# Turning float64 weights into float32 with one fewer VectorE pass, and one subtraction moved from GpSimd to VectorE

## The chip, the cores and the metric

One NeuronCore of a Trainium2 chip runs the whole program. The metric is the time of one execution on the device in microseconds (us), lower is better. The engines are TensorE (PE, with its weight loads listed apart as PEld), VectorE (DVE), ScalarE (ACT), GpSimd (POOL) and SyncE (SP), which here issues all DMAs. Each engine works through its own queue in order; semaphores hold an instruction until what it reads is there.

## The reference

Three parts follow each other: attention with keys and values averaged over 8 positions, a feed-forward layer with a rational function, and a gated feed-forward layer. Batch 8, 8 heads, 576 positions, head size 64, so 4608 tokens of 512 values; hidden sizes 2048 and 1536.

```python
k_p = k.reshape(B, H, Sp, pool, D).mean(axis=3)          # pool = 8, Sp = 72; v_p likewise
scores = scale * np.matmul(q, k_p.transpose(0, 1, 3, 2))
attn = softmax(scores); attn_out = attn @ v_p            # -> x, 4608 x 512
h = x @ w_in                                             # 512 -> 2048
P = a[0] + a[1]*h + a[2]*h**2 + a[3]*h**3
Q = 1.0 + np.abs(b[0])*np.abs(h) + np.abs(b[1])*h**2
x = (P / (Q + 1e-06)) @ w_out                            # 2048 -> 512
gate = 1.0 / (1.0 + np.exp(-(x @ w_gate))); val = x @ w_val
out = (gate * val) @ w_out2                              # 512 -> 1536 -> 512
```

The five weight matrices arrive as float64 (drawn as float32, then multiplied by a float64 scalar). The kernel reads each number as two 32-bit words and makes float32 of it by itself.

## The kernel before

**Precision by two parts.** Every large product is done with each operand split into a high part (fp32r) and a low part (what the rounding lost); a product is three matmuls (`mm3`, L485 to L487). So every weight tile needs a conversion from float64 and then a split.

**Conversion of one weight tile** (128 x 512 float64; the high words are `raw[:, :, 1]`, the low words `raw[:, :, 0]`, so each is read and written with a stride of two words). `conv1a` (ScalarE): L90 multiplies the high word, read as float32, by 2^-112, which brings the exponent into the range that float32 uses; L92 turns the low word into an integer of its top bits. `conv1b`: on VectorE, L98 shifts the result of L90 left by 3 into a scratch tile `wx`, which loses the sign, and L100 (here called the merge) takes the sign bit of the unshifted word and ORs it in; on GpSimd, L102 adds the integer of the low word. `conv2` splits: L117 (ScalarE) copies to the high part, L118 subtracts to get the low part, on GpSimd unless another engine is handed over.

**Who converts what, and when.** The first weights (`wi` from w_in, `wo` from w_out) have 16 tiles each. They are converted while the first 16 steps of the rational layer run: `weights_a(p)` (L748) does at the end of step p the split of `wi` p+3 and of `wo` p, then `conv1a` of `wi` p+5 and `wo` p+2, then loads. `conv1b` of these is put off to `gap()` (L783) in the middle of the next step. `weights_a` also runs in the lead-in steps before step 0, where the first attention tiles are made. The weights of the gated layer are converted in the background in steps 16 to 111 (`background`, L194): 12 units, three conversions each, 36 in all; `conv2` of these stays on GpSimd.

**One step n** (L770 to L794; 144 in all, 16 for each block of 512 tokens): PE computes `h` of one 128-wide slice of the hidden layer (`g1`, 12 matmuls), then attention's `psx`, then the second product of step n-3 (`g2`, 12 matmuls, `acc`), then scores and transposes of attention (`sc`, `pta`). VectorE does `rational1` (L528 to L530), the conversions of `gap()`, `rational3` (L542 to L544) and, for an attention tile, the low part of x (L420), the row maximum and difference (L369, L371) or the sum and its reciprocal (L384 to L387). ScalarE does three functions of h (L525 to L527), the high part of g (L510), Ln and Exp (L536, L538), and then the conversion's L117, L90 and L92. GpSimd does the low part of g (L513), the conversion's L102 and L118, and attention's products (L388, L334, L349). The order on each engine is the order in which the program writes the instructions (`tc.manual_schedule()`).

After step 143 comes the gated layer, which has no conversions.

Of the kernel before, what the change touches and what calls it, by code (L numbers as in the profile page):

```python
# [9 lines left out]
F32 = mybir.dt.float32  # L10
F32R = mybir.dt.float32r
I32 = mybir.dt.int32
U32 = mybir.dt.uint32
AF = mybir.ActivationFunctionType
ALU = mybir.AluOpType
# [20 lines left out]
def attention_moe_glu_kernel(ctx: ExitStack, tc: tile.TileContext, q, k, v, w_in, w_out, ca, cb, w_gate, w_val, w_out2, out):  # L36
    nc = tc.nc
# [24 lines left out]
    scale = 1.0 / math.sqrt(D)  # L62
# [13 lines left out]
    def new_tmp(name, tag="m", bufs=3):  # L76
        return rot.tile([P, 512], F32, tag=tag, name=name, bufs=bufs)
# [6 lines left out]
    def conv1a(*raws):  # L84

        for raw in raws:
            hw, lw = raw[:, :, 1], raw[:, :, 0]


            nc.scalar.activation(hw.bitcast(F32), hw.bitcast(F32), AF.Copy, scale=2.0 ** -112)  # L90

            nc.scalar.activation(lw, lw.bitcast(U32), AF.Copy, scale=2.0 ** -29)  # L92

    def conv1b(*raws):

        ws = [(raw[:, :, 1], raw[:, :, 0], new_tmp("wx").bitcast(I32)[:, :raw.shape[1]]) for raw in raws]
        for hw, lw, x in ws:
            nc.vector.tensor_scalar(out=x, in0=hw, scalar1=3, scalar2=None, op0=ALU.logical_shift_left)  # L98
        for hw, lw, x in ws:
            nc.vector.scalar_tensor_tensor(out=hw, in0=hw, scalar=-2 ** 31, in1=x, op0=ALU.bitwise_and, op1=ALU.bitwise_or)  # L100
        for hw, lw, x in ws:
            nc.gpsimd.tensor_tensor(out=hw, in0=hw, in1=lw, op=ALU.add)  # L102

    between = []
# [1 line left out]
    def conv1(*raws):  # L106
        conv1a(*raws)
        between.append(lambda: conv1b(*raws))
# [6 lines left out]
    def conv2(raw, wh, wl, eng=nc.gpsimd):  # L115
        t = raw[:, :, 1].bitcast(F32)
        nc.scalar.activation(wh, t, AF.Copy)  # L117
        eng.tensor_tensor(out=wl, in0=t, in1=wh.bitcast(F32), op=ALU.subtract)  # L118
# [7 lines left out]
    def slot(tag, dtype, name, pool=None):  # L126
        shape = [P, 2, 4 * P] if dtype is F32R else [P, 4 * P, 2]
        return (pool or wp).tile(shape, dtype, tag=tag, name=name)
# [8 lines left out]
    wi, wo, wi_raw, wo_raw = {}, {}, {}, {}  # L137
# [10 lines left out]

    def wi_conv2(f):
        wi[f] = slot(f"wi{f}", F32R, "wi")  # L150
        conv2(wi_raw.pop(f), wi[f][:, 0], wi[f][:, 1])

    def wo_load(f):
        wo_raw[f] = slot(f"wo{f + 1}", I32, "woraw") if f + 1 < FS else slot(f"st{(f + 1 - FS) % 5}", I32, "woraw", stage)
# [74 lines left out]
    with tc.manual_schedule():  # L229
# [29 lines left out]
        units, raws, loaded = [], {}, [0]  # L259
# [202 lines left out]
        for b in range(1, B):  # L462
            e0, e1 = max(at[first[b - 1]], -2), at[last[b - 1]]
            for c in range(2 * NCH):
                w, f = (("k", pool_k), ("v", pool_v))[c // NCH]
# [282 lines left out]
        def weights_a(p):  # L748

            for ahead, f, n in ((3, wi_conv2, NF1), (0, wo_conv2, NF1), (5, wi_conv1, NF1), (2, wo_conv1, NF1),  # L750
                                (8, wi_load, NF1), (5, wo_load, NF1)):
                if 0 <= p + ahead < n:
                    f(p + ahead)
# [16 lines left out]
        for n in range(N1):  # L770
# [24 lines left out]
            x = n - (N1 - NF1)  # L795
# [79 lines left out]
```

## Time and profile before

| | us |
|---|---|
| median of 3 runs (1896.67 to 1898.65) | 1896.74 |
| profiled execution: its own time | 1894.58 |
| its span, from first to last instruction | 1892.7 |

| engine, whole span | busy us | share |
|---|---|---|
| PE | 1804.6 | 95% |
| PEld | 1564.4 | 83% |
| DVE | 1242.5 | 66% |
| ACT | 943.0 | 50% |
| POOL | 896.4 | 47% |

Busy is the union of an engine's instructions. The shares are means over stages that differ: the first 45 us are attention's lead-in, from there to about 200 us the 16 steps run that convert the first weights, up to about 860 us the steps with background conversions, up to about 1000 us steps without any, and then the gated layer. The tables by stretch, further down, tell the stages apart. In a row of the timeline the first number is the start in us from the start of the span and the second the duration; what follows "out<-in" are the tiles by the names of the program; in brackets stands how long the engine was idle before and what ended that.

### The profile page before, as it was taken

The page shows a single profiled execution, that of the slowest core. Times are in us where ns is not written, and L with a number is a line of the kernel's source. Part 1 is how long each engine was busy: PE and PEld are TensorE (multiplying, and loading weights), DVE is VectorE, ACT ScalarE, POOL GpSimd, SP SyncE. Part 2 cuts the span into 40 slices and gives each one's busy share as a digit, 9 for nine tenths or more (in the row PEclk, how much of TensorE's full clock was granted, in tenths as well). Part 3 has the DMA queues.
Part 4 walks back from the last instruction along what each step waited for, and adds up shares of the span by engine and source line. Part 5 has one row for each costly group of instructions (what it writes and reads, how often), then busy time and mean ns, then how long its engine had stood idle before and what let it go on. Part 6 is the DMA issues. An engine that isn't in the chain of part 4 may idle for free.

```text
span 1892.7 us, 25138 instructions
## 1 busy us (share of the span) xinstructions
PE 1804.6 (95%) x8936; PEld 1564.4 (83%) x8936; DVE 1242.5 (66%) x1847; ACT 943.0 (50%) x1754; POOL 896.4 (47%) x855
## 2 busy tenths in 40 slices
PE   5578999999999999999999999999999999999999
PEld 4467788787777788788887999998998998998997
DVE  7999999999998899988778543343334333333331
ACT  4777777677676777776666422222222222222221
POOL 6768556565564665653224234334235225235231
PEclk9799999999999999999999999999999999999999
DMA  7343355343544553443154574574573664663661
GB/s 247 131 153 120 107 191 187 135 171 135 186 159 156 192 176 137 168 148 119 56 196 150 190 236 153 166 235 133 184 228 123 211 211 129 222 201 112 206 203 43
DMA packets 123117, 312.56 MB, mean 165 GB/s; under 512 B 11504, under 2 KB 43248, under 8 KB 122992
## 3 DMA queue, kind: packets, MB, share of 16 engines
q1 hardware_dynamic: 122992, 310.95, 48.7%
q8 instruction: 71, 1.16, 0.2%
q14 instruction: 54, 0.44, 0.1%
HBM read 257.95 MB, written 52.95 MB: 164 GB/s over the span
## 4 chain that ended last, share of the span: by engine, by line
PE 67%; DVE 21%; ACT 4%; issue 4%; DMA 2%; POOL 2%; SPq 0%; ACTq 0%; POOLq 0%; DVEq 0%
PE h L485 13%; PE h L487 12%; PE h L486 12%; PE acc L485 3%; PE acc L487 3%; PE acc L486 3%; PE accA L722 3%; PE accA L723 3%; PE h L722 3%; PE h L723 3%; PE accA L721 3%; PE h L721 3%; DVE u L528 3%; PE psx L413 3%; DVE y L544 3%
## 5 line engine op out<-in xcount | busy, mean ns | idle before, releaser
L658 DVE TENSOR_TENSOR t<-h,t 128x384 f32<-128x384 f32 x360 | 200.7, 557 | 387.0 <-ACT t L666 276.2
L513 POOL TENSOR_TENSOR g<-y,g 128x512 fp32r<-128x512 f32 x144 | 190.6, 1324 | 245.7 <-ACT g L510 186.7
L711 POOL TENSOR_TENSOR t<-t 128x384 f32<-128x384 f32 x72 | 84.4, 1172 | 448.9 <-issue 253.7
L485 PE MATMUL h<-xs,wi 128*128 128x512 f32 x576 | 234.4, 407 | 11.8 <-DVE xs L420 5.2
L485 PE MATMUL acc<-g,wo 128*128 128x512 f32 x576 | 232.8, 404 | 2.2 <-ACT g L510 2.2
L487 PE MATMUL h<-xs,wi 128*128 128x512 f32 x576 | 229.3, 398 | 3.0 <-DVE xs L420 3.0
L486 PE MATMUL h<-xs,wi 128*128 128x512 f32 x576 | 229.2, 398 | 0.0
L487 PE MATMUL acc<-g,wo 128*128 128x512 f32 x576 | 226.0, 392 | 2.4 <-POOL g L513 2.4
L486 PE MATMUL acc<-g,wo 128*128 128x512 f32 x576 | 225.0, 391 | 0.0
L487 PE MATMUL h<-xS,wq 128*128 128x384 f32 x576 | 193.1, 335 | 0.0
L485 PE MATMUL h<-xS,wq 128*128 128x384 f32 x576 | 192.9, 335 | 0.0
L486 PE MATMUL h<-xS,wq 128*128 128x384 f32 x576 | 192.7, 335 | 0.0
L528 DVE SCALAR_TENSOR_TENSOR u<-s,coef,u 128x512 f32<-128x512 f32 x144 | 132.1, 918 | 32.2 <-ACT u L526 31.9
L485 PE MATMUL h<-xA,wq 128*128 128x384 f32 x432 | 149.0, 345 | 0.0
L544 DVE SCALAR_TENSOR_TENSOR y<-u,y 128x512 f32<-128x512 f32 x144 | 143.9, 999 | 4.9
L487 PE MATMUL h<-xA,wq 128*128 128x384 f32 x432 | 144.7, 335 | 0.0
L486 PE MATMUL h<-xA,wq 128*128 128x384 f32 x432 | 144.6, 335 | 0.0
L485 PEld LDWEIGHTS h<-xs,wi 128*128 128x128 f32 x576 | 111.3, 193 | 39.1 <-DVE xs L420 4.2
L525 ACT ACTIVATE s<-h 128x512 f32<-128x512 f32 x144 | 85.0, 590 | 110.4 <-PE h L487 110.3
L542 DVE SCALAR_TENSOR_TENSOR u<-u,h 128x512 f32<-128x512 f32 x144 | 98.5, 684 | 56.0 <-ACT h L538 54.3
L487 PEld LDWEIGHTS h<-xs,wi 128*128 128x128 f32 x576 | 111.1, 193 | 27.9 <-DVE xs L420 3.5
L485 PEld LDWEIGHTS acc<-g,wo 128*128 128x128 f32 x576 | 108.5, 188 | 27.9 <-ACT g L510 2.6
(122 smaller groups left out, 4300.2 us busy)
## 6 DMA issues: line engine op xcount, KB each, us to landing
wq<-w2d SPq DMA_DIRECT2D x252, 512.0 KB, 4.3
wo<-wod SPq DMA_DIRECT2D x88, 512.0 KB, 3.8
w2d<-wq SPq DMA_DIRECT2D x36, 512.0 KB, 2.9
x2d<-o SPq DMA_DIRECT2D x36, 256.0 KB, 2.4
out_dram<-o SPq DMA_DIRECT2D x36, 256.0 KB, 2.0
raw<-in_k_dram SPq DMA_DIRECT2D x32, 256.0 KB, 2.8
raw<-in_q_dram SPq DMA_DIRECT2D x32, 256.0 KB, 2.7
raw<-in_v_dram SPq DMA_DIRECT2D x32, 256.0 KB, 3.1
```

The lines of the kernel that those rows point to most:

```text
L485: nc.tensor.matmul(out_, wl, xh, start=start, stop=False, skip_group_check=on)
L486: nc.tensor.matmul(out_, wh, xh, start=False, stop=False, skip_group_check=on)
L487: nc.tensor.matmul(out_, wh, xl, start=False, stop=stop, skip_group_check=on)
L513: eng.tensor_tensor(out=g[:, 1], in0=y, in1=g[:, 0].bitcast(F32), op=ALU.subtract)
L525: nc.scalar.activation(s, h, AF.Square)
L528: nc.vector.scalar_tensor_tensor(out=u, in0=s, scalar=coef[:, 5:6], in1=u, op0=ALU.mult, op1=ALU.add)
L542: nc.vector.scalar_tensor_tensor(out=u, in0=u, scalar=ONE, in1=r, op0=ALU.add, op1=ALU.mult)
L544: nc.vector.scalar_tensor_tensor(out=y, in0=u, scalar=-2.0, in1=y, op0=ALU.add, op1=ALU.mult)
L658: nc.vector.tensor_tensor(out=out_, in0=a, in1=b, op=ALU.add)
L721: nc.tensor.matmul(a[t], gh, wt[:, 0], start=(f == 0), stop=False)
L722: nc.tensor.matmul(a[t], gh, wt[:, 1], start=False, stop=False)
L723: nc.tensor.matmul(a[t], gl, wt[:, 0], start=False, stop=(f == NF2 - 1))
```

## The change

The multiplication on ScalarE (L90) becomes a leaky one, `Prelu`, with alpha 2^32: positive numbers get the factor 2^-112 as before, negative ones 2^-80. The exponent field of a negative result then has one more bit set, two places below the top; the shift by 3, which pushes out the old sign, moves that bit into the sign's place. So the shift alone gives the right word, and it is done in place: the merge (the old L100) and the scratch tile `wx` go. This holds for all 68 conversions, 32 of the first weights and 36 in the background. Apart from that, `wi_conv2` hands `nc.vector` to `conv2`: the low parts (L118) of the 16 `wi` tiles are computed on VectorE, not on GpSimd. Those of `wo` and of the background stay.

```diff
-            nc.scalar.activation(hw.bitcast(F32), hw.bitcast(F32), AF.Copy, scale=2.0 ** -112)
+            nc.scalar.activation(hw.bitcast(F32), hw.bitcast(F32), AF.Prelu, scale=2.0 ** -112, alpha=2.0 ** 32)
             nc.scalar.activation(lw, lw.bitcast(U32), AF.Copy, scale=2.0 ** -29)
     def conv1b(*raws):
-        ws = [(raw[:, :, 1], raw[:, :, 0], new_tmp("wx").bitcast(I32)[:, :raw.shape[1]]) for raw in raws]
-        for hw, lw, x in ws:
-            nc.vector.tensor_scalar(out=x, in0=hw, scalar1=3, scalar2=None, op0=ALU.logical_shift_left)
-        for hw, lw, x in ws:
-            nc.vector.scalar_tensor_tensor(out=hw, in0=hw, scalar=-2 ** 31, in1=x, op0=ALU.bitwise_and, op1=ALU.bitwise_or)
-        for hw, lw, x in ws:
+        ws = [(raw[:, :, 1], raw[:, :, 0]) for raw in raws]
+        for hw, lw in ws:
+            nc.vector.tensor_scalar(out=hw, in0=hw, scalar1=3, scalar2=None, op0=ALU.logical_shift_left)
+        for hw, lw in ws:
             nc.gpsimd.tensor_tensor(out=hw, in0=hw, in1=lw, op=ALU.add)
...
     def wi_conv2(f):
         wi[f] = slot(f"wi{f}", F32R, "wi")
-        conv2(wi_raw.pop(f), wi[f][:, 0], wi[f][:, 1])
+        conv2(wi_raw.pop(f), wi[f][:, 0], wi[f][:, 1], nc.vector)
```

In the changed file two empty lines more stand ahead of L90, so its Prelu is L92, its low-word copy L94, its shift L100; L102 and all later numbers are as before.

What VectorE has in a row in one step with both conversions, before (step 2; `wiraw` and `woraw` are raw tiles of w_in and w_out, `wx` the scratch tile):

```order
L528 SCALAR_TENSOR_TENSOR u<-s,coef,u 128x512
L529 TENSOR_TENSOR y<-h,y 128x512
L530 SCALAR_TENSOR_TENSOR y<-y,coef,h 128x512
L98 TENSOR_SCALAR wx<-wiraw 128x512
L100 SCALAR_TENSOR_TENSOR wiraw<-wiraw,wx 128x512
L98 TENSOR_SCALAR wx<-woraw 128x512
L100 SCALAR_TENSOR_TENSOR woraw<-woraw,wx 128x512
L542 SCALAR_TENSOR_TENSOR u<-u,h 128x512
L543 SCALAR_TENSOR_TENSOR y<-y,coef,h 128x512
L544 SCALAR_TENSOR_TENSOR y<-u,y 128x512
```

The same place of VectorE in the changed program:

```order
L118 TENSOR_TENSOR wi<-wiraw,wi 128x512
L528 SCALAR_TENSOR_TENSOR u<-s,coef,u 128x512
L529 TENSOR_TENSOR y<-h,y 128x512
L530 SCALAR_TENSOR_TENSOR y<-y,coef,h 128x512
L100 TENSOR_SCALAR wiraw<-wiraw 128x512
L100 TENSOR_SCALAR woraw<-woraw 128x512
L542 SCALAR_TENSOR_TENSOR u<-u,h 128x512
L543 SCALAR_TENSOR_TENSOR y<-y,coef,h 128x512
L544 SCALAR_TENSOR_TENSOR y<-u,y 128x512
```

The two merges are gone, the two shifts (now L100) stand side by side, and the low part of a `wi` tile comes in at the end of the step before, right ahead of L528.

GpSimd at the end of step 1 and in step 2, before (L388 is attention's product, L513 the low part of g):

```order
L388 TENSOR_TENSOR e<-e,r 64x576
L118 TENSOR_TENSOR wi<-wiraw,wi 128x512
L118 TENSOR_TENSOR wo<-woraw,wo 128x512
L513 TENSOR_TENSOR g<-y,g 128x512
L102 TENSOR_TENSOR wiraw<-wiraw 128x512
L102 TENSOR_TENSOR woraw<-woraw 128x512
```

The same place of GpSimd in the changed program:

```order
L388 TENSOR_TENSOR e<-e,r 64x576
L118 TENSOR_TENSOR wo<-woraw,wo 128x512
L513 TENSOR_TENSOR g<-y,g 128x512
L102 TENSOR_TENSOR wiraw<-wiraw 128x512
L102 TENSOR_TENSOR woraw<-woraw 128x512
```

Only the subtraction of `wi` is gone there; nothing else moved. The order on PE, ScalarE and SyncE is that of before, instruction for instruction; ScalarE has its two table loads (L232 and L696) at the same places.

## Rows read from the trace of the kernel before

**Rows 1.** Busy time by stretch: us, then each engine's busy us (instructions).

```profile
core 0: us, PE busy (x) PEld busy (x) DVE busy (x) ACT busy (x) POOL busy (x), PEclk, DMA share, GB/s
...
60.00:200.00 140.00, 106.58 (x471) 86.56 (x472) 137.79 (x179) 100.03 (x178) 103.99 (x91) 0.87 0.37 126
215.00:860.00 645.00, 624.90 (x3023) 512.16 (x3022) 586.85 (x885) 460.57 (x859) 388.43 (x403) 1.00 0.45 162
860.00:1000.00 140.00, 139.87 (x660) 115.95 (x659) 111.20 (x168) 89.82 (x157) 43.46 (x32) 1.00 0.35 124
```

**Rows 2.** The chain that ended last, 60 to 200 us, by line.

```profile
by line: DVE wx L98 17.3%; DVE woraw L100 13.0%; DVE y L544 8.4%; DVE u L528 8.2%; DVE wiraw L100 8.0%; DVE y L530 6.9%; DVE y L543 6.2%; DVE y L529 6.1%; DVE u L542 5.5%; issue 5.3%; DVE e L371 2.5%; DVE kp L317 2.0%; DVE r L384 1.9%; DVE 
```

**Rows 3.** VectorE's groups, 17 to 205 us: xcount | busy us, mean ns | idle before.

```profile
L544 DVE SCALAR_TENSOR_TENSOR y<-u,y 128x512 f32<-128x512 f32 x16 | 23.6, 1474 | 0.6
L100 DVE SCALAR_TENSOR_TENSOR woraw<-woraw,wx 128x512 int32<-128x512 int32 x16 | 21.7, 1358 | 0.5
L98 DVE TENSOR_SCALAR wx<-wiraw 128x512 int32<-128x512 int32 x16 | 18.9, 1179 | 0.5 <-ACT wiraw L90 0.5
L100 DVE SCALAR_TENSOR_TENSOR wiraw<-wiraw,wx 128x512 int32<-128x512 int32 x16 | 16.8, 1049 | 0.5
L98 DVE TENSOR_SCALAR wx<-woraw 128x512 int32<-128x512 int32 x16 | 12.8, 800 | 0.0
```

**Rows 4.** Lines 98 and 100 by themselves: duration in ns, min/median/max, and starts.

```profile
L98 DVE TENSOR_SCALAR wx<-woraw x16: 416/422/2223, 37.5 to 191.0; 128x512 int32<-128x512 int32 x16
...
L100 DVE SCALAR_TENSOR_TENSOR wiraw<-wiraw,wx x16: 693/695/2028, 22.4 to 166.6; 128x512 int32<-128x512 int32 x16
```

**Rows 5.** Timeline around 113 us, VectorE and GpSimd.

```profile
112.64 1.30 POOL L118 TENSOR_TENSOR wi<-wiraw,wi 128x512 fp32r<-128x512 f32 x1
...
112.97 1.25 DVE L98 TENSOR_SCALAR wx<-wiraw 128x512 int32<-128x512 int32 x1
...
113.90 1.49 POOL L118 TENSOR_TENSOR wo<-woraw,wo 128x512 fp32r<-128x512 f32 x1
...
114.25 1.68 DVE L100 SCALAR_TENSOR_TENSOR wiraw<-wiraw,wx 128x512 int32<-128x512 int32 x1
```

**Rows 6.** Timeline around 50 us, VectorE and GpSimd.

```profile
49.72 0.31 POOL L335 TENSOR_TENSOR vp<-raw 64x64 f32<-64x64 f32 x1
50.00 1.28 POOL L118 TENSOR_TENSOR wi<-wiraw,wi 128x512 fp32r<-128x512 f32 x1
50.10 6.25 DVE L544 SCALAR_TENSOR_TENSOR y<-u,y 128x512 f32<-128x512 f32 x1
...
54.51 1.29 POOL L118 TENSOR_TENSOR wo<-woraw,wo 128x512 fp32r<-128x512 f32 x1
```

**Rows 7.** GpSimd's groups, 17 to 205 us: xcount | busy us, mean ns | idle before.

```profile
L118 POOL TENSOR_TENSOR wo<-woraw,wo 128x512 fp32r<-128x512 f32 x15 | 22.6, 1504 | 0.0
L513 POOL TENSOR_TENSOR g<-y,g 128x512 fp32r<-128x512 f32 x15 | 21.8, 1453 | 10.5 <-DVE y L529 10.5
L118 POOL TENSOR_TENSOR wi<-wiraw,wi 128x512 fp32r<-128x512 f32 x16 | 21.0, 1310 | 0.0
L102 POOL TENSOR_TENSOR woraw<-woraw 128x512 int32<-128x512 int32 x16 | 16.6, 1038 | 9.3 <-DVE woraw L100 8.7 <-ACT coef L768 0.7
```

**Rows 8.** ScalarE's groups: two of 17 to 205 us, and a table load.

```profile
L527 ACT ACTIVATE y<-h,coef 128x512 f32<-128x512 f32 x17 | 13.2, 778 | 0.0
L90 ACT ACTIVATE woraw<-woraw 128x512 f32<-128x512 f32 x16 | 10.7, 671 | 0.0
...
L232 ACT ACT_TABLE_LOAD x1 | 1.3, 1283 | 0.8 <-PEq L851 0.8
```

**Rows 9.** Timeline from step 1 to step 2, ScalarE and VectorE.

```profile
65.55 0.69 ACT L526 ACTIVATE u<-h,coef 128x512 f32<-128x512 f32 x1
...
66.28 0.75 DVE L528 SCALAR_TENSOR_TENSOR u<-s,coef,u 128x512 f32<-128x512 f32 x1
```

**Rows 10.** Who waited for whom, 17 to 205 us: total us, times, longest.

```profile
PE pta L395 <- POOL e L388: 33.4, 6, 12.1
```

## The prediction

> **What bounds the kernel now.** I read the stretches first, since the shares of the whole span mix stages. From 60 to 200 us VectorE is busy 137.79 of 140 us and TensorE 106.58, at a mean granted clock of 0.87; from 215 to 860 us TensorE is busy 624.90 of 645 and VectorE 586.85; without conversions (860 to 1000 us) TensorE is busy 139.87 of 140 [rows 1]. So the change can act in two places: strongly in the first 16 steps, where VectorE has no time left, and weakly in the background steps, where TensorE idles 20.1 us in all. Then the chain: from 60 to 200 us it runs almost wholly over VectorE, and three of its lines are the shift and the merges of the conversion, 17.3 + 13.0 + 8.0 = 38% [rows 2]. The gated layer has no conversions and stays as it is.
>
> Last, I ask why these VectorE instructions take so long. A shift takes 0.42 us and a merge 0.69 when nothing is in the way [rows 4], but in the first steps their means are 0.80 to 1.18 and 1.05 to 1.36 us, and L544, with both inputs in SBUF too, has 1.47 [rows 3]. The timeline shows the cause: L98 arrives at 112.97, while GpSimd is in L118 until 113.94, and ends at 114.22, one free duration after that; GpSimd's next L118 takes 1.49 instead of 1.30; L100 comes at 114.25 and waits that one out [rows 5]. These VectorE instructions and GpSimd's exclude each other. It can be worse: L544 at 50.10 waits through five GpSimd instructions in a row, to 56.35 [rows 6].
>
> On that wait the Trainium skill, "SBUF — State Buffer", section "Who interferes with whom", says that a VectorE instruction with two SBUF inputs, or in a mode that uses both ports, and a GpSimd instruction that reads SBUF exclude each other, and that the second one blocks until the first has finished. It speaks against moving L118: on VectorE it is itself such an instruction. Rows 5 agree with it; rows 6 don't, since there the wait lasts for five. By the rule no wait could exceed one GpSimd instruction, step 0 would have nothing to win from a shorter run, and my slower rival (D) could not occur.
>
> **The change part by part, first 16 steps and lead-in.** All in VectorE time, 17 to 205 us.
>
> 1. Merges out: 21.7 + 16.8 = 38.5 us for 32 [rows 3]. Their waits go with them. Certain.
>
> 2. Low parts of `wi` in: 16 instructions of a form that VectorE doesn't have now; nearest is the merge (two SBUF inputs, one with a stride of two, 512 elements): 0.69 free [rows 4], 1.36 on the mean where it always runs into GpSimd [rows 3]. So 11.0 to 21.8; I take the mean of the `wi` merges, 1.05, as L118 stands behind other work as they do: 16.8 us. It waits for ScalarE's L117, which ScalarE reaches before VectorE has done L542 to L544, so I add no wait. Queued behind it on VectorE is L528 of the next step, and behind that ScalarE's Ln and all of `rational3`; a wait here would move the whole step.
>
> 3. Shifts: 18.9 + 12.8 = 31.7 us now [rows 3]; free they would be 32 x 0.42 = 13.4, so 18.3 us are waiting. The second shift of a step now starts right behind the first, before GpSimd's add of the first tile can start, and GpSimd's run ahead of the first is shorter by one L118 of 1.31 us [rows 7]. I take half: -9 (0 to -18). The destination is now strided. The merge writes with that stride at 0.69 [rows 4], so at worst a free shift costs 0.69: +0.27 x 32 = +8.6. I take 0.42, the row with the same operation and input.
>
> 4. L544: 23.6 - 16 x 0.69 = 12.6 us of waiting now [rows 3]. With the merges gone the two adds and L118 of `wo` stand on GpSimd without gaps, so L544 may find one more add (1.04 us [rows 7]) ahead of it; but L118 of `wi` is no longer there, and the run of rows 6 loses two of its five. I take 0 (-8 to +8).
>
> 5. Prelu in L90's place: Copy takes 0.671 us; the dearest function of one input on this engine takes 0.778, with two operands read per partition [rows 8]. Prelu has none of these, so I take 0.671; at the other end 32 x 0.107 = 3.4 us on an engine busy 100.03 of 140 us [rows 1]. Less than Copy is excluded by nothing in the rows, but no path could use it: 0 to +3. The order shows no new table load.
>
> Sum: -38.5 + 16.8 - 9 + 0 = -30.7 us of VectorE time.
>
> 6. What is late next. ScalarE: step 1 has nothing to give, since L526 ends at 66.24 and L528 starts at 66.28 [rows 9]. TensorE: in six places the transposes wait for attention's L388 on GpSimd, 33.4 us in all [rows 10]; behind L388 stand transposes, scores and the next h, so a step after such a place can shorten by only part of what VectorE saves. I count the one step as lost and half of the six: 4 of 16, a quarter. So 0.75 x 30.7 = 23 us arrive. GpSimd is no bound: it loses 21.0 us [rows 7].
>
> **Background, 215 to 860 us.** 36 merges go. TensorE's idle time there is 20.1 us, against 0.1 in 140 us without conversions, so at most 19.5 can be won. Conversions stand in 3 of 8 steps, and the merge is about 0.69 of the 0.69 + 1.0 us that one takes (1.0 is the mean of the shifts in rows 3): 19.5 x 3/8 x 0.41 = 3 us (0 to 7).
>
> Gain 23 + 3 = 26 us. The profiled execution took 1894.58 us (span 1892.7), 2.2 under the median, so 1868.6 there and 1896.7 - 26 = **1870.7 us** for the median.
>
> **Rivals.**
>
> A, the port takes much back: the waits move instead of going. L118 at 21.8, shifts keep their 18.3, L544 +8: -38.5 + 21.8 + 8 = -8.7, times 0.75 = 6.5 us, 1890. For it: rows 5, where one wait follows another and the loop closes over both engines. Against: GpSimd's own load falls by 21 us, and fewer instructions compete.
>
> B, the in-place shift is slow: +8.6, so 22.1 x 0.75 + 3 = 19.6, 1877. The Trainium skill, "VectorE: DVE Perf Modes", section "What auto-detection actually checks", asks for SBUF operands and matching outer dimensions, not for unit stride, before it takes two elements per cycle; by it the shift stays at 0.42. No row shows a strided destination in that operation.
>
> C, more than forecast: all 18.3 us of the shifts' waits and 8 of L544's go too, and TensorE's clock rises because it idles less: 30.7 + 9 + 8 = 47.7, times 0.75 = 36, and 7 behind: 1854.
>
> D, slower: L118 on VectorE gets behind whole GpSimd runs, as L544 in rows 6. It is then 1.50 (L118 of `wo`) + 1.45 (L513) + 0.69 = 3.64 us each [rows 4, 7], 58 us for 16, against 38.5 gained; with L544 at +8 the sum is +28, and as it stands right on VectorE's path nothing of it is hidden: 1925. It decides from 38.5 / 16 = 2.41 us per L118, that is a wait of 1.7. For it: rows 6. Against: that run follows an instruction on 64 partitions (L335), and in rows 5, with full ones, VectorE gets in after a single one.
>
> E, the change doesn't do what it says: Prelu is missing in the loaded table and each use brings two loads. 68 x 2 x 1.283 [rows 8] = 174 us, 2071. The order has only the two loads of before.
>
> **How the numbers follow.** Chances: forecast (1862 to 1876) 0.58, A 0.14, B 0.10, C 0.11, D 0.06, E 0.01. The range goes from near C's end to near A's: 1856 to 1888; half of A, D, E and a little of C lie outside, 0.17. About 0.2%, 3.8 us, is what a measurement of this kernel can tell from no change. Faster by more: the forecast, B, C and most of A, 0.90. The same: the rest of A, 0.04. Slower: D, E, 0.06.
>
> **What would show it right or wrong.** In the profile after: 32 shifts in the first steps, mean 0.5 to 0.8 us, minimum 0.42 (0.69 would be B); 16 low parts on VectorE at about 1.05 us (3.6 would be D); ScalarE's Prelu at 0.67; the end of the first 16 steps 23 us earlier; VectorE still the busiest of that stretch but with some idle time before L528, put down to ScalarE or TensorE; L544 of step 0 well under 6.25. Wrong would be a gain in the gated layer, a TensorE that is busy 98% in the first steps, or a gain there under 10 us with all durations as said: then the quarter in step 6 was too small.

## The result and the profile after

The changed kernel takes 1864.74 us (median of 4 runs, 1862.82 to 1865.53), the one before beside it 1896.7: a ratio of 0.983, 95% interval 0.9813 to 0.9847, so 32 us less. The prediction was 1870.7. The profiled execution took 1865.44 us, with a span of 1863.6.

The same three stretches as in [rows 1], now of the changed kernel (us, then the busy us of each engine with its instructions, TensorE's granted clock, DMA share, GB/s):

```profile
60.00:200.00 140.00, 120.51 (x559) 98.11 (x560) 125.72 (x185) 108.99 (x197) 93.29 (x85) 0.91 0.42 142
215.00:860.00 645.00, 632.78 (x3092) 521.91 (x3091) 572.52 (x864) 466.05 (x871) 386.64 (x401) 1.00 0.47 166
860.00:1000.00 140.00, 135.10 (x608) 110.72 (x607) 110.13 (x153) 88.27 (x151) 46.36 (x31) 0.98 0.35 121
```

VectorE is no longer busy all the time from 60 to 200 us, and TensorE has 14 us more work in it. Fixed windows cover other work once a kernel is shorter, though, so the two kernels are better cut at the same steps: at the first instruction (L528) of VectorE in step 0, 16 and 112. Before:

```profile
45.85:204.24 158.39, 118.71 (x516) 95.48 (x515) 154.52 (x199) 112.69 (x200) 115.41 (x104) 0.87 0.38 131
204.24:861.06 656.82, 636.06 (x3082) 521.16 (x3082) 597.01 (x902) 469.21 (x875) 393.79 (x407) 1.00 0.46 162
```

After:

```profile
41.95:185.88 143.93, 114.00 (x517) 92.03 (x516) 130.55 (x186) 111.03 (x200) 98.84 (x94) 0.89 0.42 144
185.88:829.57 643.69, 629.71 (x3074) 519.11 (x3075) 574.15 (x866) 467.60 (x875) 391.55 (x407) 1.00 0.47 165
```

Step 16 starts 18.4 us earlier (3.9 of them already at step 0), the 96 steps with background conversions take 13.1 less, and everything behind step 112 takes 2.4 more (the span is 29.1 shorter, not 31.5). The median moved by 32, the profiled executions by 29.1.

VectorE's groups of the changed kernel, 17 to 185 us, which answer to [rows 3] (xcount | busy us, mean ns | idle before):

```profile
L528 DVE SCALAR_TENSOR_TENSOR u<-s,coef,u 128x512 f32<-128x512 f32 x16 | 23.7, 1479 | 11.1 <-ACT u L526 11.0
L544 DVE SCALAR_TENSOR_TENSOR y<-u,y 128x512 f32<-128x512 f32 x16 | 18.8, 1178 | 0.6
L100 DVE TENSOR_SCALAR wiraw<-wiraw 128x512 int32<-128x512 int32 x16 | 13.7, 853 | 0.0
L118 DVE TENSOR_TENSOR wi<-wiraw,wi 128x512 fp32r<-128x512 f32 x16 | 12.7, 791 | 0.0
...
L100 DVE TENSOR_SCALAR woraw<-woraw 128x512 int32<-128x512 int32 x16 | 10.4, 651 | 0.0
```

The row of before that has to stand beside the first of these, and that the prediction left out (17 to 205 us):

```profile
L528 DVE SCALAR_TENSOR_TENSOR u<-s,coef,u 128x512 f32<-128x512 f32 x17 | 14.1, 830 | 2.6 <-ACT u L526 2.6
```

Single durations (ns, min/median/max) of the new shift, of L118 on VectorE, and of the Prelu, answering to [rows 4, 8]:

```profile
L100 DVE TENSOR_SCALAR wqraw<-wqraw x36: 419/1250/1553, 206.4 to 825.3; 128x512 int32<-128x512 int32 x36
L100 DVE TENSOR_SCALAR wiraw<-wiraw x16: 415/513/1458, 21.9 to 153.5; 128x512 int32<-128x512 int32 x16
L100 DVE TENSOR_SCALAR woraw<-woraw x16: 416/420/1697, 37.1 to 173.9; 128x512 int32<-128x512 int32 x16
...
L118 DVE TENSOR_TENSOR wi<-wiraw,wi x16: 632/686/1220, 30.6 to 165.0; 128x512 fp32r<-128x512 f32 x16
...
L92 ACT ACTIVATE wiraw<-wiraw x16: 657/674/692, 19.3 to 146.3; 128x512 f32<-128x512 f32 x16
```

The chain of the changed kernel, 60 to 185 us, by line, which answers to [rows 2]:

```profile
by line: DVE u L528 13.2%; DVE y L544 8.9%; DVE y L530 7.8%; DVE y L529 6.9%; issue 4.7%; DVE woraw L100 4.7%; DVE y L543 4.3%; PE h L485 4.0%; DVE wiraw L100 3.9%; DVE u L542 3.8%; PE h L486 3.8%; PE h L487 3.6%; DVE wi L118 3.5%; PE sc L3
```

The conversion had 38% of the chain and has 12 (4.7 + 3.9 + 3.5). TensorE's matmuls appear in it, and L528 has taken the first place. Why, the timeline of VectorE and GpSimd at the end of step 0 shows (start, duration):

```profile
48.51 0.94 DVE L118 TENSOR_TENSOR wi<-wiraw,wi 128x512 fp32r<-128x512 f32 x1
49.48 5.15 DVE L528 SCALAR_TENSOR_TENSOR u<-s,coef,u 128x512 f32<-128x512 f32 x1
...
48.98 0.65 POOL L335 TENSOR_TENSOR vp<-raw 64x64 f32<-64x64 f32 x1
49.59 1.03 POOL L102 TENSOR_TENSOR wiraw<-wiraw 128x512 int32<-128x512 int32 x1
50.59 1.03 POOL L102 TENSOR_TENSOR woraw<-woraw 128x512 int32<-128x512 int32 x1
51.58 1.28 POOL L118 TENSOR_TENSOR wo<-woraw,wo 128x512 fp32r<-128x512 f32 x1
52.83 1.25 POOL L513 TENSOR_TENSOR g<-y,g 128x512 fp32r<-128x512 f32 x1
```

It is the wait of [rows 6] again: L544 of step 0 has lost it (it takes 0.69 at 46.44), but GpSimd's run behind the 64-partition L335 is still there, four instructions long, and L528 of step 1 falls into it. It ends at 54.63, 0.55 us after the run's last instruction; the wait of [rows 6] also ends 0.55 after the run's (54.51 + 1.29 = 55.80; 56.35).

### The profile page after: what moved, and what is told of

It reads as the page before. It is cut to its first block, busy times and chain, and to the rows that moved or that the text cites. A ratio compares the mean times of both kernels' runs of the same rounds, so it can differ in the third digit from the quotient of the medians.

```text
span 1863.6 us, 25047 instructions
## 1 busy us (share of the span) xinstructions
PE 1794.3 (96%) x8936; PEld 1559.6 (84%) x8936; DVE 1192.5 (64%) x1795; ACT 940.0 (50%) x1754; POOL 873.2 (47%) x839
## 4 chain that ended last, share of the span: by engine, by line
PE 72%; DVE 14%; ACT 5%; issue 3%; POOL 2%; DMA 2%; SPq 0%; ACTq 0%; POOLq 0%; DVEq 0%
PE h L485 14%; PE h L487 13%; PE h L486 13%; PE acc L485 4%; PE acc L487 4%; PE acc L486 4%; PE psx L413 3%; DVE u L528 3%; PE h L722 3%; PE h L723 3%; PE h L721 3%; PE accA L722 3%; PE accA L723 3%; PE accA L721 3%; DVE y L530 2%
## 5 line engine op out<-in xcount | busy, mean ns | idle before, releaser
L513 POOL TENSOR_TENSOR g<-y,g 128x512 fp32r<-128x512 f32 x144 | 187.7, 1304 | 265.6 <-ACT g L510 204.7
L485 PE MATMUL h<-xs,wi 128*128 128x512 f32 x576 | 231.7, 402 | 6.7 <-DVE xs L420 3.8
L487 PE MATMUL h<-xs,wi 128*128 128x512 f32 x576 | 227.0, 394 | 0.3 <-DVE xs L420 0.3
L486 PE MATMUL h<-xs,wi 128*128 128x512 f32 x576 | 227.0, 394 | 0.0
L528 DVE SCALAR_TENSOR_TENSOR u<-s,coef,u 128x512 f32<-128x512 f32 x144 | 140.8, 978 | 49.6 <-ACT u L526 49.2
L544 DVE SCALAR_TENSOR_TENSOR y<-u,y 128x512 f32<-128x512 f32 x144 | 136.3, 947 | 4.9
L485 PEld LDWEIGHTS h<-xs,wi 128*128 128x128 f32 x576 | 109.9, 191 | 31.9 <-DVE xs L420 4.6
L485 PEld LDWEIGHTS acc<-g,wo 128*128 128x128 f32 x576 | 108.5, 188 | 27.9 <-ACT g L510 2.6
L487 PEld LDWEIGHTS acc<-g,wo 128*128 128x128 f32 x576 | 108.6, 189 | 27.6 <-POOL g L513 3.6
```

Of the source, the lines that this page charges most:

```text
L485: nc.tensor.matmul(out_, wl, xh, start=start, stop=False, skip_group_check=on)
L486: nc.tensor.matmul(out_, wh, xh, start=False, stop=False, skip_group_check=on)
L487: nc.tensor.matmul(out_, wh, xl, start=False, stop=stop, skip_group_check=on)
L513: eng.tensor_tensor(out=g[:, 1], in0=y, in1=g[:, 0].bitcast(F32), op=ALU.subtract)
L528: nc.vector.scalar_tensor_tensor(out=u, in0=s, scalar=coef[:, 5:6], in1=u, op0=ALU.mult, op1=ALU.add)
L544: nc.vector.scalar_tensor_tensor(out=y, in0=u, scalar=-2.0, in1=y, op0=ALU.add, op1=ALU.mult)
```

## The experiments

**The two parts apart.** The sign step alone, with L118 of `wi` left on GpSimd:

```diff
-        conv2(wi_raw.pop(f), wi[f][:, 0], wi[f][:, 1], nc.vector)
+        conv2(wi_raw.pop(f), wi[f][:, 0], wi[f][:, 1])
```

> The changed kernel, but with the low parts of wi (L118) left on GpSimd; so it has the sign step alone. Port theory (the first 16 steps are bound by what VectorE's port-sharing instructions and GpSimd's take one after the other): L118 occupies the shared port for 1.31 us on GpSimd and 0.69 on VectorE, so this kernel is slower than the changed one by up to 16 x 0.62 = 10 us, I expect 4 to 8, that is 1869 to 1873. Rival (VectorE's own list of instructions is the bound, as the prediction's sum counts it): VectorE has 12.7 us less to do than in the changed kernel, of which three quarters arrive: 1855.

Measured 1865.88 us, ratio 0.9845 (0.9831 to 0.9858): 1 us above the changed kernel, too little to tell from no difference. And the other part alone, L118 moved in the kernel before:

> The kernel before, but with the low parts of wi (L118) moved to VectorE; merges and scratch tile stay. Port theory: the port gets free of 16 x 0.62 = 10 us and the runs on GpSimd get shorter, so faster than before by 3 to 8 us, 1889 to 1894. Rival (VectorE's list alone): VectorE has 16 more instructions of 0.8 us and up, 12.7 us, three quarters arrive: 1906.

Measured 1900.85 us, ratio 1.0026 (1.0016 to 1.0035): 4 to 5 us slower. So the sign step carries the whole gain, 30 to 36 us, and moving the subtraction is worth nothing beside it. Neither account of the price fits either run: L118 on VectorE takes 0.76 us on the mean in the second run and 0.79 in the changed kernel, so it seldom waits long for GpSimd; but where VectorE is full, as before, even 0.76 seems to be more than its removal from GpSimd gives back.

**First weights and background apart.** The old sign step (Copy, shift, merge) only for the 36 background tiles, then only for the 32 first ones with L118 on GpSimd:

```diff
-            conv1(bg["raw"][r - 2])
+            conv1_old(bg["raw"][r - 2])
...
-            conv1(bg["raw"][2])
+            conv1_old(bg["raw"][2])
```

> The changed kernel, but the 36 background conversions done in the old way (Copy, shift into the scratch tile, merge). The trace after is 18.4 us ahead at step 16 and 31.5 at step 112. If the 13.1 us between come from the background merges, this kernel takes 1875 to 1878. Rival: they come from the state that the first 16 steps hand over (a backlog on TensorE and a lower granted clock, which the trace before shows until 370 us and the trace after doesn't); then it stays within 4 us of the changed kernel, 1865 to 1869.

> The kernel before in the first weights (Copy, merge, L118 on GpSimd), with the changed conversion in the 36 background tiles alone. If the background merges are worth what the traces show between steps 16 and 112, 13 us, it takes 1884; by the prediction's own term, 3 us, 1894; the rival of e3 says 1893 to 1897.

Measured 1877.92 us, ratio 0.9905 (0.9891 to 0.9918), and 1885.04, ratio 0.9943 (0.9931 to 0.9956). The background's merges are worth 13 us by the first and 11 by the second, four times the 3 of the prediction; that they come from a state handed over by the first 16 steps is out. VectorE's groups of the background steps say what it saved; before (204 to 861 us):

```profile
L98 DVE TENSOR_SCALAR wx<-wqraw 128x512 int32<-128x512 int32 x36 | 36.0, 1001 | 0.0
L100 DVE SCALAR_TENSOR_TENSOR wqraw<-wqraw,wx 128x512 int32<-128x512 int32 x36 | 25.5, 708 | 1.2
```

and after (185 to 830 us):

```profile
L100 DVE TENSOR_SCALAR wqraw<-wqraw 128x512 int32<-128x512 int32 x36 | 41.5, 1152 | 0.0
```

36.0 + 25.5 - 41.5 = 20.0 us saved, of which 13.1 arrived.

**What the merge's price is made of.** To tell VectorE's own time from its waits for GpSimd, the changed kernel got, after each of the 68 shifts, a row maximum over the same words into a scratch column that nobody reads: an instruction with one input, as long as a merge.

```diff
             nc.vector.tensor_scalar(out=hw, in0=hw, scalar1=3, scalar2=None, op0=ALU.logical_shift_left)
+            nc.vector.reduce_max(new_tmp("wx")[:, :1], hw.bitcast(F32), axis=AX.X)
```

> The changed kernel with one added VectorE instruction behind each of the 68 shifts, a maximum over the 512 words (its result isn't used): about 0.67 us, one SBUF input, so nearly as long as the merge when that was free, but no rival of GpSimd's. List theory (VectorE's own time was the price of the merge): most of the gain goes, 32 x 0.67 x 0.75 = 16 us in the first steps and 13 in the background, 1888 to 1895. Port theory (the merge was dear because it shared the port with GpSimd): a third of that or less, 1865 to 1875.

Measured 1892.21 us, ratio 0.9976 (0.9965 to 0.9987). The added instruction by itself (ns, min/median/max):

```profile
L101 DVE TENSOR_REDUCE wx<-wqraw x36: 685/686/690, 220.8 to 853.9; 128x1 f32<-128x512 f32 x36
...
L101 DVE TENSOR_REDUCE wx<-wiraw x16: 685/686/690, 22.6 to 165.2; 128x1 f32<-128x512 f32 x16
L101 DVE TENSOR_REDUCE wx<-woraw x16: 685/686/687, 38.6 to 188.1; 128x1 f32<-128x512 f32 x16
```

None of the 68 ever waits for GpSimd, and yet 27 of the 32 us are given back: 68 x 0.686 = 46.6 us of VectorE time, 0.59 of which arrives. So what the merge cost was mostly VectorE's own time; that the merge also kept GpSimd out was the small part. The Trainium skill, "SBUF — State Buffer", section "Who interferes with whom", names this kind of instruction as one that never contends on this chip; the trace agrees, with 5 ns between the shortest and the longest. One thing the run does not separate: like the merge, the row maximum also holds up GpSimd's add of the same tile, so a part of the price may be that delay.

**The order of L118 and L528.** Is the 5.15 us wait due to L118 standing right ahead of L528? The subtraction was put off into the middle of the next step:

```diff
-        conv2(wi_raw.pop(f), wi[f][:, 0], wi[f][:, 1], nc.vector)
+        raw = wi_raw.pop(f)[:, :, 1].bitcast(F32)
+        wh, wl = wi[f][:, 0], wi[f][:, 1]
+        nc.scalar.activation(wh, raw, AF.Copy)
+        between.append(lambda: nc.vector.tensor_tensor(out=wl, in0=raw, in1=wh.bitcast(F32), op=ALU.subtract))
```

> The changed kernel, but the subtraction L118 of wi is put off on VectorE from the end of a step into the gap() of the next, behind the shifts. In the trace after, L528 takes 1.48 us instead of 0.83 in the first 16 steps (23.7 against 14.1 us), right behind L118. If that order costs time (L528 stands at the head of the step's path over Ln, Exp and rational3), this kernel gains: 4 to 8 us, 1857 to 1861. Rival (the wait for GpSimd's run only goes to whichever port instruction comes next, so that the order doesn't matter): within 3 us of 1864.7.

Measured 1864.91 us (1863.12 to 1868.76): no difference. Its trace bears out the rival: L528 of step 1 still takes 4.46 us, and two more long waits of the first 16 steps go to what comes next on VectorE, a shift (2.88) and the later L118 itself (2.75).

**What makes the long waits.** Between 17 and 930 us six VectorE instructions take over 2.4 us in the changed kernel (5.15, 2.72, 4.11, 4.75, 4.99, 4.94), and six before (3.75 to 6.25). Those of the changed kernel all start in or behind an instruction of GpSimd on 64 partitions (L335 above, L388 three times, the last instruction of the mask L349 twice), and all six end 0.54 to 0.56 us after the last instruction of the run that follows it. The changed kernel has 40 such instructions, 8 of each of five kinds, as

```profile
L388 POOL TENSOR_TENSOR e<-e,r 64x576 f32<-64x576 f32 x8 | 10.2, 1274 | 19.5 <-DVE r L387 19.5
```

They were made 128 partitions wide. The upper half works on numbers that nobody reads: a second load of the same rows of v, and copies of the identity matrix for the upper half of `e` and `r`. No wait was taken away.

```diff
+                if m < P:
+                    nc.sync.dma_start(t[m:], rows[c * P:c * P + m])
...
-            t = take("v", b, c)[:m]
+            t, m = take("v", b, c), P
...
-                m = P if c < NCH - 1 else CL
+                m = P
...
+            if n < P:
+                nc.scalar.activation(e_[n:], ident[n:, :SP].unsqueeze(1).to_broadcast([P - n, H, SP]), AF.Copy)
...
+            if n < P:
+                nc.scalar.activation(r[n:], ident[n:, :H], AF.Copy)
...
-            nc.gpsimd.tensor_tensor(out=e_[:n], in0=e_[:n], in1=r[:n].unsqueeze(2).to_broadcast([n, H, SP]), op=ALU.mult)
+            nc.gpsimd.tensor_tensor(out=e_, in0=e_, in1=r.unsqueeze(2).to_broadcast([P, H, SP]), op=ALU.mult)
```

> The changed kernel, but GpSimd's instructions on 64 partitions run on 128: rows 64 to 127 of the last chunk of v are loaded twice, those of e and r of a 64-token tile are filled by two small ScalarE copies (0.7 and 0.2 us); the extra rows are not used. Theory: after an instruction on half of the partitions GpSimd's halves run apart, and VectorE gets the port only when the whole run ends. Then L528 of step 1 (5.15 us) and of step 4 (4.11) fall to 1.3 to 2.0, and no VectorE instruction of the first 16 steps waits through more than one of GpSimd's: 3 to 7 us faster, 1858 to 1862. Rival (the long waits come from when VectorE arrives, not from the half partitions): the two stay over 3.5 us, and the time is that of the changed kernel or, with the extra copies, up to 3 us more.

Measured **1848.02 us** (1847.82 to 1850.02), ratio 0.9742 (0.9729 to 0.9756): 17 us less than the changed kernel, though GpSimd, ScalarE and the DMAs have more to do. It beats both kernels. The theory was right on the waits and far too low on the time (3 to 7 us). The same place in its trace (line numbers there are up to 6 higher: L534 is L528, L337 is L335):

```profile
49.57 0.75 DVE L534 SCALAR_TENSOR_TENSOR u<-s,coef,u 128x512 f32<-128x512 f32 x1
50.24 0.68 DVE L535 TENSOR_TENSOR y<-h,y 128x512 f32<-128x512 f32 x1
...
49.05 0.65 POOL L337 TENSOR_TENSOR vp<-raw 128x64 f32<-128x64 f32 x1
49.66 1.56 POOL L102 TENSOR_TENSOR wiraw<-wiraw 128x512 int32<-128x512 int32 x1
```

L534 starts at the same time as L528 did, and takes 0.75 us instead of 5.15; this time L102 is the one that waits (1.56 for 1.03). Between 17 and 930 us no VectorE instruction takes over 1.83 us any more. Step 16 starts 11.6 us earlier than in the changed kernel, step 112 17.9. From step 0 to step 16 the windows read

```profile
42.00:174.28 132.28, 110.14 (x512) 89.39 (x512) 122.31 (x187) 112.82 (x204) 101.73 (x94) 0.92 0.46 157
```

against 143.93 us, VectorE 130.55 busy and a mean granted clock of 0.89 in the changed kernel: 8.2 us less of VectorE's busy time, and 3.4 less of its idle time. TensorE is also less at its lower clock (1.2 GHz for about 20 us of the stretch, against 31); how much of the 11.6 runs through that, no run separates.

With this and the later L118 together:

> e5 and e6 together. If both causes are real and apart from each other, the gains add: 1852 to 1858. If they are the same waits, no better than the better of the two.

Measured 1851.9 us, ratio 0.976 (0.9747 to 0.9774): 4 us worse than with the full width alone. Here the order does count, against the later place.

The two kinds of 64-partition instruction apart, first only attention's product L388, then only the averaging of v with its mask:

> The changed kernel in which only attention's product (L388), of the two kinds of GpSimd instructions on 64 partitions, is made 128 wide; the averaging of v and its mask stay. Theory: both kinds make VectorE wait, and the gain of 17 us splits: step 1's wait of 5.15 us stands behind the averaging and step 4's of 4.11 us behind L388, so about 8 here: 1857, within 4. Rival: TensorE's transposes wait for L388 alone, so nearly all 17 us are had here: 1849.

> The other half: the changed kernel in which only the averaging of v and its mask are made 128 wide; L388 stays on 64 partitions. Theory: about 9 of the 17 us, 1856, within 4, and with the run on L388 alone the two add up to 17 within 3. Rival: 1863 or more, since it is L388 that counts.

Measured 1855.53 us, ratio 0.9784 (0.9771 to 0.9798), and 1860.53, ratio 0.9807 (0.9793 to 0.982): 9 and 4 us, both kinds count, L388 more. The waits go with their kind: over 2.4 us there remain in the first run two, both behind the averaging and its mask (5.15 and 4.99), and in the second four, all behind L388 (4.11 twice, 4.75, 4.94). The sum of 13 is short of the 17 of both together by slightly more than I allowed.

**Is that gain independent of the change?** The full width in the kernel before, and in the kernel with the sign step alone (L118 of `wi` on GpSimd):

> The kernel before with GpSimd's 64-partition instructions made 128 wide, nothing of the change. Theory: the waits behind such instructions are independent of the change and as dear without it: 17 us less than before, 1880, within 4. Rival 1: before, GpSimd's runs are longer by one subtraction of 1.3 us, so these waits cost more, and 25 us go: 1872. Rival 2: before, VectorE is full in the first steps whatever it waits for, and only the 6 us of the background are to be had: 1891.

> The changed kernel with GpSimd's 64-partition instructions made 128 wide (1848.0 us), and with the low parts of the wi tiles back on GpSimd, so of the change only the sign step is left. Theory: the place of these 16 subtractions is worth nothing here either, since what VectorE saves (16 x 0.79 = 12.6 us) GpSimd's longer runs take back as waits: 1848, within 3. Rival: without the long waits VectorE's own time is what counts, and 12.6 us less of it, at three quarters, gives 9 us: 1839.

Measured 1891.02 us, ratio 0.9968 (0.9957 to 0.9979), and 1858.24, ratio 0.9796 (0.9782 to 0.9809). The six medians in us:

| | 64 partitions | all 128 |
|---|---|---|
| before | 1896.3 to 1897.6 | 1891.0 |
| sign step alone | 1865.9 | 1858.2 |
| sign step and L118 of `wi` on VectorE | 1864.7 | 1848.0 |

The width alone is worth 6 us before, 8 with the sign step, and 17 with both parts. Read the other way, moving L118 is worth 1 us with the waits and 10 without them. Both of my expectations for these two runs failed in their sizes, and the rival of the second (1839) too. Only the second rival of the first, that before VectorE is full whatever it waits for, came out at its 1891, but not for its reason. It gave all 6 us to the background; in the trace step 16 starts 2.0 us earlier, the background takes 3.4 less, and what follows 1.5 more. And where it says that VectorE is full, its busy time in the first 16 steps fell by 5.0 us (154.52 to 149.50), of which 2.8 came back as idle time. The wait of [rows 6] has shrunk to one GpSimd instruction:

```profile
50.28 1.75 DVE L550 SCALAR_TENSOR_TENSOR y<-u,y 128x512 f32<-128x512 f32 x1
...
50.19 1.29 POOL L118 TENSOR_TENSOR wi<-wiraw,wi 128x512 fp32r<-128x512 f32 x1
```

In the run with the sign step alone, full width, the waits from 17 to 190 us say why L118 belongs on VectorE then (total us, times, longest):

```profile
DVE u L534 <- ACT u L532: 18.6, 9, 5.2
```

and of TensorE, 40 to 110 us:

```profile
PE h L491 <- POOL wi L118: 4.8, 1, 4.8
```

TensorE waits 4.8 us for the low part of `wi`, which GpSimd does behind the averaging of v; h of step 1 comes late, so ScalarE's L532, so VectorE's L534, whose longest wait of 5.2 us this is. With L118 on VectorE no matmul waits for `wi`, and the 18.6 us are

```profile
DVE u L534 <- ACT u L532: 6.6, 5, 2.3
```

At full width the move puts step 1 3.3 us ahead (52.83 to 49.57) and step 16 8.5; how the other waits of L534 went stays open. In the changed kernel the same move puts step 1 3.4 us ahead of the kernel with the sign step alone (49.48 to 52.84 us), and then L528 takes 5.15 us, behind GpSimd's run: by step 2 (62.08 to 61.35) the gain is gone. That shows one way in which the waits took the gain back. It is not the whole account: in step 2 the other kernel has such a wait (L528, 4.18), and from there to step 16 (185.88 to 184.92) the two were not followed step by step.

## Why the prediction was right, and where only by luck

The time fell within the forecast's own band (1862 to 1876), but two terms were off in opposite directions: the first 16 steps gave 18.4 us, not 23, and the background 13.1, not 3.

1. **Merges out**: as said; all 32 and 36 are gone.
2. **L118 on VectorE**: +12.7 us, not +16.8. It takes 0.79 on the mean, nearer to the free end of the bounds. The stand-in, the merge of `wi` in the middle of a step, ran into GpSimd no more often (6 of 16 over 0.75 us, as here) but waited longer, up to 2.03 us against 1.22.
3. **Shifts**: 18.9 + 12.8 in [rows 3] have become 13.7 + 10.4, -7.6 for -9. In place and strided, a free one takes 0.415 us: rival B is out.
4. **L544 at 0**: wrong in its own size, 16 x (1.178 - 1.474) = -4.7 us, and wrong in what it left out. The waits behind GpSimd's runs did not stay with L544, and the sum had no term for the instruction that they would go to: L528, 16 x (1.479 - 0.830) = +10.4 us.
5. **Prelu**: 0.67 us, as Copy; no table load was added. Rival E is out.

   The measured sum is -38.5 + 12.7 - 7.6 - 4.7 + 10.4 = -27.7, near the -30.7 of the prediction because 2 and 4 hide the 10.4.
6. **A quarter lost**: a third was. 18.4 / 27.7 = 0.66. That ScalarE and TensorE would be late next was right: VectorE's idle time before L528 rose from 2.6 to 11.0 us, all put down to L526.

**Background.** The failing step is the last one, 19.5 x 3/8 x 0.41. It took TensorE's idle time as a budget and spread it evenly over the steps. The steps show no such evenness: of the 12.8 us that the 96 steps gained, counted from one start of h to the next, 10.5 lie in three steps of eight, the one with the third conversion of a unit and the two behind it, and none in the two steps that do the first two conversions. By VectorE's own time the total was to be had: 20.0 us saved, 13.1 arrived, 0.66, the share of the first steps. But that share is no rule for a single conversion: the first two of each unit save 12.0 of the 20.0 us, and nothing arrives in their steps; the third saves 8.0, and 10.5 arrive in its step and the two behind it. That the two totals give the same share may be chance. Of the 13.1, TensorE's idle time accounts for 20.8 - 14.0 = 6.8, more than the 3 forecast; the other 6.3 are in its busy time. Some of that is in h, as these rows of the two pages show for the whole span (before, then after):

```profile
L485 PE MATMUL h<-xs,wi 128*128 128x512 f32 x576 | 234.4, 407 | 11.8 <-DVE xs L420 5.2
```

```profile
L485 PE MATMUL h<-xs,wi 128*128 128x512 f32 x576 | 231.7, 402 | 6.7 <-DVE xs L420 3.8
```

Of the 6.3, by estimate 1.7 are the 8 matmuls by which the two windows differ (3082 and 3074, at some 0.2 us), and 1.7 are TensorE's clock: before, it is at 1.2 GHz for 3.4 us from 359 us on, after 3.3 us in which TensorE was busy for 0.76; in the changed kernel it is at 2.4 GHz in all of these 96 steps. The clock is not the cause, since the run with the new background alone has such a stretch too (at 576 us) and still gains 11.4 us in these steps. What the rest of the matmuls waited for inside their busy time, the trace does not show, and it stays open. The 19.5 as a bound held; what failed is how it was shared out, and that TensorE's idle time was taken for all there was to win.

**Rivals.** A (the port takes much back) had one mechanism right, a wait that moves on, but not the price: L118 at 0.79, not 1.36, and the row maximum, which never waits, gives 27 us back. C missed, as the waits did not go; its other half came true in part, since TensorE's mean granted clock in the first 16 steps rose from 0.87 to 0.89 (1.2 GHz for about 41 us before, 31 after). How much of the 18.4 us runs through that, no run separates. D, L118 behind whole GpSimd runs, did not happen to L118 (1.22 at most); it happened to the instruction after it, twice in the first steps (5.15 and 4.11 us). The prediction's point against D, that a run of this kind follows an instruction on 64 partitions, is what the full width bore out.

**The rule on the port.** The prediction set it against [rows 6]: one blocks until the other has finished, so no wait could exceed one GpSimd instruction. With all 128 partitions the rule holds: 1.75 us in place of 6.25 and 0.75 in place of 5.15. The Trainium skill, "GPSIMD Engine Reference", section "2.1 Instruction dispatch", says that GpSimd's cores serve 16 partitions each and begin the next instruction as soon as their own share of the last is done. By that, cores left without work by a 64-partition instruction would run ahead of the others, and one or another would hold the port until the run is over. The runs agree with it in both respects, that the wait ends with the run and that it needs the half-filled instruction; the cores themselves no run here shows. How a wait ends is the same for one instruction and for a run: in [rows 5] the shift ends 0.28 us after GpSimd's L118 (not a whole free duration of 0.42, as the prediction read it) and the merge 0.54 after the next.

**What was to be seen.** The shifts' means are 0.85 and 0.65, together 0.75 (said: 0.5 to 0.8), L544 of step 0 is at 0.69, TensorE is busy 114.00 of 143.93 us in the first 16 steps (79%; 98% would have been wrong), and the gated layer gained nothing.

## What to carry to other kernels

Where an engine is late in a stretch, price an edit in that engine's time and take a share of it, rather than by what another engine idles. Here the share was two thirds in both stretches and 0.59 for the row maximum; it is a total over many steps, and by single steps it ran from nothing to more than all. When a wait shrinks because its victim moves, name the next victim and give it a term. And where VectorE waits through a whole run of GpSimd, look at how many partitions the run's first instruction has: filling it up with numbers nobody reads was worth 17 us in the changed kernel and 6 in the one before, and only with it did the moved subtraction pay.

## What the runs showed of the hardware that I had not expected

After a GpSimd instruction on 64 partitions, a VectorE instruction with two SBUF inputs, or the shift, waited until GpSimd's run had ended (the longest took 2.7 to 6.25 us and ended some 0.55 us after the run's last instruction, the shift 0.28); with all of GpSimd's instructions on 128 partitions no VectorE instruction took over 1.83 us between 17 and 930 us, and none sat through more than one whole instruction of GpSimd's. An in-place shift of 128x512 words at a stride of two takes 0.415 us, as into a dense tile (0.416). A Prelu with its own slope takes 0.67 us, what Copy takes.
